# Attention, gated MLP and convolved MLP on one core: two V chunks normalised later, and the attention pairs' factors moved behind two more evictions

## The chip, the core and the metric

The kernel runs on one core of one Trainium2 chip. The metric is the device time of one execution in microseconds (us), as the median of several runs; the profile is one further execution, recorded by the hardware profiler. TensorE (PE) multiplies matrices, VectorE (DVE), ScalarE (ACT) and GpSimd (POOL) work on elements, SyncE (SP) issues most of the DMA transfers.

## What is computed

Three stages follow each other, on 4 batches of 576 positions. Attention has 8 heads of 64, a causal window of 128 positions and a linear bias. Its output, 576 x 512, goes through a gated MLP with a spatial product over the positions, and that result through a second MLP with a convolution over three positions.

```python
# attention, per batch and head
scores = where(0 <= rel < 128, q @ k.T / 8 - slope * rel, -1e9)
attn = exp(scores - max) / (sum + 1e-9)
x = attn @ v                                  # heads side by side: 576 x 512
# gated MLP
h = gelu_tanh(x @ w_in)                       # 576 x 1024
u, v = h[:, :512], h[:, 512:]
v_n = (v - mean) / sqrt(var + 1e-6) * g_ln    # over the 512 columns
v_s = w_sg @ v_n + b_sg[:, None]              # 576 x 576 product over positions
x = x + (u * v_s) @ w_out
# second MLP
h = relu(x @ w_in2)
out = (h * sigmoid(conv3(h, conv_w))) @ w_out2
```

The weights arrive as float64 and are narrowed to float32 on the chip, word by word.

## The kernel before, in words

Every float32 matrix is split into a high and a low part, and a product is made of three matmuls, high by high, high by low and low by high. A row of heads is handled two at a time, as a pair; a batch has four pairs. The attention of batch b+1 is interleaved with the gated MLP of batch b, so that PE always has something to multiply. The second MLP follows at the end and is not touched here.

The order of the work is written out by hand in `_steps()` (lines 45 to 135) as a string of short steps. A letter names the step, the numbers behind it the batch and the pair or chunk:

- `L`, `M` load q, k and V of a pair. `C` makes its scores on PE (tile `sc`) and adds the bias and takes the maximum on DVE; this is called masking here (`masked`, line 451, nine instructions to a pair, each followed by a short read of the accumulator). `E` takes the exponentials on ACT (tile `t`, nine to a pair, through `act`, line 186). `N` (`a_norm`, line 495) adds 1e-9 to the sums, takes the reciprocal on DVE (tile `r`, lines 498 and 499) and multiplies the nine blocks by it, on DVE or POOL (`scaled`, line 242). These multiplications are called the factors. `T` transposes the weights on PE (tile `pT`, 13 matmuls, line 515) and copies them out of the accumulator memory on ACT or DVE (tile `ph`). `A` multiplies them by V (tile `o`, 52 matmuls). `X` splits the result into `xg`.
- `V` (`m_v`, line 753 on) makes one of five chunks of the normalised v: matmuls (`psv`), the gelu on ACT, mean and variance on DVE (`bs`, `ba`), the reciprocal root on POOL (`rs`, lines 784 and 785), then on DVE `v` minus the mean times the root (line 786), and the split into high (ACT) and low part (DVE), tile `vn`. Chunk 4 has the last 64 positions.
- `U` makes the gate's other factor u (`psu`, then a gelu on ACT). `G` makes the product over positions (`pss`, 14 matmuls to one of four column blocks of a half), which DVE moves out with the gain and the bias (line 843, called the eviction here). POOL multiplies by u and the result is split into `gh` and `gl`. `W` multiplies by `w_out` (`pso`, 12 matmuls), and DVE adds the residual.
- `g`, `o`, `a` narrow pieces of weights: five DVE instructions (lines 324 to 331) on a tile `wa` that has two buffers, then a high part on ACT and a low part on POOL (tile `wo`) or both on POOL (`wh`, `wa`).

In the stretch that counts here the accumulator memory has two banks for `psv`, `psu`, `pss` and `pso` together and six for the attention, so the third product of a run waits until the first has been moved out. Each engine takes its instructions in the order that the scheduler leaves; `add_manual_dep` with `follow` sets an order within one engine without a wait. ACT's activations that need a table are chained in program order in this way.

The pairs of the next batch are called pair 1 to pair 4 below, the four products of the first half (256 columns) G0.0 to G0.3, and those of the second half (320 columns) G1.0 to G1.3; W0.0 to W0.3 are the output products of the first half.

Of the kernel before, what the change touches and what calls it, by code (L numbers as in the profile page):

```python
# [15 lines left out]
P = 128  # L16
# [37 lines left out]
def _steps():  # L54
# [5 lines left out]
    def scores(p):  # L60
        return [f"C{of(p)}"]
# [10 lines left out]
    def loads(p):  # L72
        return [f"L{of(p)}", f"M{of(p)}"]
# [12 lines left out]
    for b in range(B - 1):  # L86
# [5 lines left out]
        if b == 0:  # L92
            uv = ["g0", "g1", V[2], "g2", "o0.0", U[0][3], "g3", "o0.1", V[4]] + loads(p) + ["g4", "o1.0"] + scores(p) + ["o1.1", V[3], "o2.0", "o2.1"]
            uv += loads(p + 1) + U[1][:2] + ["o3.0"] + scores(p + 1) + ["o3.1"] + loads(p + 2) + U[1][2:] + scores(p + 2)
        else:
            uv = V[:2] + loads(p) + scores(p) + V[2:] + loads(p + 1) + scores(p + 1) + U[0] + loads(p + 2) + U[1][:1] + scores(p + 2) + U[1][1:]
        T, A = ([f"{x}{of(p + i)}" for i in range(4)] for x in "TA")
        gw = weigh(p) + G[0] + weigh(p + 1) + G[1][:1] + loads(p + 3) + T[:1] + G[1][1:2] + W[0][:1] + A[:1] + halves(p)
        gw += weigh(p + 2) + W[0][1:2] + T[1:2] + W[0][2:] + A[1:2] + scores(p + 3) + halves(p + 1) + weigh(p + 3) + T[2:3] + G[1][2:3]
# [35 lines left out]
def attention_gmlp_glu_kernel(  # L135
# [359 lines left out]
    def a_norm(b, m):  # L495
        s = st8[b, m]
        r = apool.tile([P, 9], F32, tag="r", name="r", bufs=2)
        nc.vector.tensor_scalar_add(r, s["sm"], 1e-9)
        nc.vector.reciprocal(r, r)
        book("dve", 170)  # L500
        for j, i in ORDER:
            e, c, _ = weights(s["t"], m, j, i)
            scaled(e, e, r[:, c : c + 1], ON["norm"])
# [39 lines left out]

    copies, masks, last_sg = [], [], []

# [203 lines left out]
    def m_v(b, j):  # L749
# [22 lines left out]
        v = mpool.tile([P, HF], F32, tag="v", name="v", bufs=NV)
        if j < 4:
            act(v, ps, AF.Gelu_apprx_tanh)
        else:
            copy(v[:r], ps[r:], True, "act")
            tt(v[:r], ps[:r], v[:r], ALU.add, "dve")
            act(v[:r], v[:r], AF.Gelu_apprx_tanh)
        bs, ba, rs = small(6, "bs"), small(2, "ba"), small(1, "rs")
        book("dve", 1200)  # L780
        nc.vector.bn_stats(bs[:r], v[:r])
        nc.vector.bn_aggr(ba[:r], bs[:r])
        book("pool", 800)
        nc.gpsimd.tensor_scalar(rs[:r], ba[:r, 1:2], 1.0, 1e-6, op0=ALU.mult, op1=ALU.add)
        nc.gpsimd.tensor_tensor(rs[:r], rs[:r], mhalf[:r], op=ALU.pow)
        nc.vector.tensor_scalar(v[:r], v[:r], ba[:r, 0:1], rs[:r], op0=ALU.subtract, op1=ALU.mult)
        split(hi[:r], lo if j < 4 else hi[64:], v[:r], "vn first")
# [39 lines left out]
    def m_sg(b, half, d):  # L827
# [44 lines left out]
    def constants(i):  # L872
# [12 lines left out]
        k=constants, l=z_load, v=z_vload, c=z_scores, e=z_exp, n=z_norm, t=z_transpose, z=z_av, j=w_in_load, L=a_load, M=a_vload, C=a_scores, E=a_exp, N=a_norm, T=a_transpose, A=a_av,  # L885
        X=a_xsplit, V=m_v, U=m_u, G=m_sg, W=m_wo, i=w_in_piece, g=w_sg_piece, o=w_out_piece, a=w2_piece,
    )
# [231 lines left out]
```

## Time and profile before

| what | value |
|---|---|
| median of 3 runs | 542.7 us |
| lowest and highest of them | 542.19 and 546.43 us |
| the profiled execution's own time | 543.29 us |
| its span, first to last instruction | 541.1 us |
| time outside the span | 2.2 us |
| mean granted TensorE clock | 0.997 of full |

PE is busy in nearly all of the span, so the time is read from the places where it isn't. The timeline merges neighbouring instructions of one kind into one row: start, length, engine, line, operation, tiles, shape and count, and in brackets how long the engine stood idle before the row and what ended that. The windows view gives, for each stretch, the busy time and count of each engine and the granted clock.

### The profile page before, as it was taken

The page shows a single profiled execution, that of the slowest core. Times are in us where ns is not written, and L with a number is a line of the kernel's source. Part 1 is how long each engine was busy: PE and PEld are TensorE (multiplying, and loading weights), DVE is VectorE, ACT ScalarE, POOL GpSimd, SP SyncE. Part 2 cuts the span into 40 slices and gives each one's busy share as a digit, 9 for nine tenths or more (in the row PEclk, how much of TensorE's full clock was granted, in tenths as well). Part 3 has the DMA queues.
Part 4 walks back from the last instruction along what each step waited for, and adds up shares of the span by engine and source line. Part 5 has one row for each costly group of instructions (what it writes and reads, how often), then busy time and mean ns, then how long its engine had stood idle before and what let it go on. Part 6 is the DMA issues. An engine that isn't in the chain of part 4 may idle for free.

```text
span 541.1 us, 11980 instructions
## 1 busy us (share of the span) xinstructions
PE 520.7 (96%) x4548; PEld 474.7 (88%) x4548; DVE 367.7 (68%) x959; ACT 258.7 (48%) x673; POOL 243.2 (45%) x383
## 2 busy tenths in 40 slices
PE   8997989999998999999999999999999999999997
PEld 6776879898898988989988999998998999999887
DVE  4999798754878875879767688687567354654300
ACT  6694578342458451376534434452554333444310
POOL 2444238542146363246453344245586545465500
PEclk9999989999999999999999999999999999999999
DMA  8974541433261765243643433902202100100011
GB/s 290 394 241 175 150 121 52 148 113 98 89 201 37 218 187 190 82 124 92 173 144 115 155 101 131 337 13 52 75 21 81 66 22 19 42 21 27 33 39 59
DMA packets 33209, 63.93 MB, mean 118 GB/s; under 512 B 3968, under 2 KB 13952, under 8 KB 33152
## 3 DMA queue, kind: packets, MB, share of 16 engines
q1 hardware_dynamic: 33008, 63.04, 35.8%
q8 instruction: 36, 0.59, 0.5%
q14 instruction: 21, 0.17, 0.1%
q10 hardware_dynamic: 144, 0.13, 0.1%
HBM read 48.47 MB, written 14.68 MB: 117 GB/s over the span
## 4 chain that ended last, share of the span: by engine, by line
PE 62%; DVE 14%; ACT 9%; POOL 7%; DMA 5%; issue 3%; SPq 0%; ACTq 0%; DVEq 0%; POOLq 0%
PE psg L213 31%; PE psv L213 7%; PE pso L213 6%; PE psu L213 5%; PE o L213 4%; ACT t L186 3%; PE pss L213 3%; PE sc L213 3%; POOL t L242 3%; PE pT L515 2%; DMA w<-in_w_in_dram 2%; DVE t L451 1%; DVE wa L330 1%; DMA kq<-in_qk_dram 1%; DVE wa L328 1%
## 5 line engine op out<-in xcount | busy, mean ns | idle before, releaser
L213 PEld LDWEIGHTS psg<-x2g,w 128*128 128x128 f32 x768 | 103.1, 188 | 2.4 <-ACT hb L973 0.7
L213 PE MATMUL psg<-x2g,w 128*128 128x256 f32 (+1 forms) x768 | 104.6, 294 | 0.6 <-ACT hb L973 0.5
L213 PE MATMUL psg<-wout,gh 128*128 128x512 f32 (+1 forms) x272 | 80.1, 378 | 0.0
L186 ACT ACTIVATE t<-t,st 128x192 f32<-128x192 f32 (+1 forms) x144 | 61.9, 431 | 15.0 <-DVE st L451 15.0
L213 PE MATMUL pss<-wsg,vn 128*128 128x256 f32 (+1 forms) x448 | 63.6, 298 | 3.6 <-DVE t L843 3.0
L213 PEld LDWEIGHTS pss<-wsg,vn 128*128 128x128 f32 x448 | 60.5, 190 | 4.7 <-DVE t L843 4.0
L977 DVE SCALAR_TENSOR_TENSOR cc<-hb,cw,cc 128x576 f32<-128x576 f32 x32 | 26.6, 832 | 46.9 <-POOL cc L242 46.9
L213 PEld LDWEIGHTS psg<-wout,gh 128*128 128x128 f32 x272 | 49.8, 188 | 8.7
L213 PE MATMUL psu<-xg,win 128*128 128x320 f32 (+1 forms) x384 | 54.2, 298 | 2.6 <-ACT win L222 1.7
L213 PEld LDWEIGHTS psu<-xg,win 128*128 128x128 f32 x384 | 51.7, 188 | 3.7 <-ACT win L222 1.8
L213 PE MATMUL pso<-gh,wo 128*128 128x256 f32 (+1 forms) x256 | 51.8, 300 | 0.5 <-DVE t L843 0.5
L213 PE MATMUL psg<-wout,gl 128*128 128x512 f32 (+1 forms) x136 | 50.9, 378 | 0.0
L213 PE MATMUL psv<-win,xg 128*128 128x512 f32 x192 | 47.6, 398 | 0.9 <-DVE wa L328 0.9
L242 POOL TENSOR_SCALAR cc<-hb,cw 128x576 f32<-128x576 f32 x32 | 28.3, 885 | 42.7 <-ACT hb L973 42.7
L451 DVE CUSTOM_DVE_ANT_0 t<-sc,tab 128x192 f32<-128x192 f32 (+1 forms) x144 | 40.4, 335 | 5.4 <-PE sc L213 5.0
L973 ACT ACTIVATE hb<-psg 128x576 f32<-128x576 f32 x32 | 20.7, 651 | 47.5 <-PE psg L213 45.0
L213 PEld LDWEIGHTS psv<-win,xg 128*128 128x128 f32 x192 | 35.5, 188 | 8.7 <-ACT win L222 1.0
L231 DVE TENSOR_TENSOR gg<-cc,hb 128x576 f32<-128x576 f32 x32 | 30.1, 943 | 17.2 <-ACT cc L186 17.0
L213 PEld LDWEIGHTS pso<-gh,wo 128*128 128x128 f32 x256 | 40.3, 188 | 1.7 <-DVE t L843 1.2
L213 PE MATMUL pso<-gl,wo 128*128 128x256 f32 (+1 forms) x128 | 36.9, 301 | 1.3 <-POOL gl L231 0.6
L231 POOL TENSOR_TENSOR t<-t,u 128x256 f32<-128x256 f32 (+1 forms) x32 | 27.2, 854 | 18.6 <-DVE t L843 18.4
L231 POOL TENSOR_TENSOR gl<-gg,gh 128x512 fp32r<-128x512 f32 x24 | 33.7, 1404 | 0.6
(101 smaller groups left out, 960.4 us busy)
## 6 DMA issues: line engine op xcount, KB each, us to landing
V<-in_v_dram SPq DMA_DIRECT2D x12, 704.0 KB, 4.7
x2s<-x2d SPq DMA_DIRECT2D x16, 288.0 KB, 2.9
w<-in_w_in_dram SPq DMA_DIRECT2D x8, 512.0 KB, 7.5
w<-in_w_out_dram SPq DMA_DIRECT2D x16, 256.0 KB, 3.2
w<-in_w_in_dram SPq DMA_DIRECT2D x16, 256.0 KB, 2.8
wout<-w2d SPq DMA_DIRECT2D x8, 512.0 KB, 6.0
q<-in_q_dram SPq DMA_DIRECT2D x12, 320.0 KB, 4.0
out_dram<-ot SPq DMA_DIRECT2D x15, 256.0 KB, 2.0
```

The lines of the kernel that those rows point to most:

```text
L186: ins = nc.scalar.activation(*args, **kw)
L213: return nc.tensor.matmul(out, lhsT, rhs, start=start, stop=stop, **kw)
L231: return (nc.vector if eng == "dve" else nc.gpsimd).tensor_tensor(dst, a, b, op=op)
L242: e.tensor_scalar(dst, src, col, 1.0, op0=ALU.mult, op1=ALU.mult)
L328: tc.keep_in_program_order(clamp.tensor_scalar(f(a), f(a), W_LOW, W_HIGH, op0=ALU.max, op1=ALU.min))
L330: nc.vector.scalar_tensor_tensor(a, high, 0xC0000000, a, op0=ALU.bitwise_and, op1=ALU.bitwise_or)
L451: nc.vector.tensor_tensor_reduce(e, bank, table, scale=-SCALE, scalar=3e38, op0=ALU.add, op1=ALU.min, accum_out=mx)
L515: ins = nc.tensor.transpose(ps[:, i * P : (i + 1) * P], src, ident)
L973: nc.scalar.activation(h[:, 1 : S + 1], ps[:, 256 : 256 + S], AF.Relu)
L977: nc.vector.scalar_tensor_tensor(cc, h[:, 0:S], cw[:, 0, c : c + 1], cc, op0=ALU.mult, op1=ALU.add)
```

## The change

Three things are done. In batch 0 the normalisation of V chunks 4 and 3 is cut out of `m_v` into a step of its own (`s`, `m_vnorm`), and both stand behind pair 2's scores; a dependency puts their first DVE instruction behind pair 2's last mask. In batches 1 and 2 the sums and reciprocals of pair 1 and pair 2 are put behind the eviction that was last in program order, that is of G0.3 and of G1.0. In the order of the steps of batches 0 to 2, `N` of pair 1 moves behind G0.3, `N` of pair 2 behind G1.0, and `T` of pair 1 behind G1.1. Lines behind the edits stand one to sixteen lower in the new file.

```diff
-            uv += loads(p + 1) + U[1][:2] + ["o3.0"] + scores(p + 1) + ["o3.1"] + loads(p + 2) + U[1][2:] + scores(p + 2)
+            uv += loads(p + 1) + U[1][:2] + ["o3.0"] + scores(p + 1) + ["s0.4", "s0.3", "o3.1"] + loads(p + 2) + U[1][2:] + scores(p + 2)
...
+        (E1, N1), (E2, N2) = (([x] for x in weigh(q)) for q in (p, p + 1))
...
-        gw = weigh(p) + G[0] + weigh(p + 1) + G[1][:1] + loads(p + 3) + T[:1] + G[1][1:2] + W[0][:1] + A[:1] + halves(p)
+        gw = E1 + G[0] + N1 + E2 + G[1][:1] + N2 + loads(p + 3) + G[1][1:2] + T[:1] + W[0][:1] + A[:1] + halves(p)
...
-        nc.vector.tensor_scalar_add(r, s["sm"], 1e-9)
+        ins = nc.vector.tensor_scalar_add(r, s["sm"], 1e-9)
+        if m < 2 and b > 0:
+            tc.add_manual_dep(ins.ins, last_gate[0].ins.name, follow, reason="behind pss")
...
+        vs[b, j] = (v, ba)
+        if b or j < 3:
+            m_vnorm(b, j)
+
+    vs = {}
+
+    def m_vnorm(b, j):
+
+        v, ba = vs.pop((b, j))
+        r = P if j < 4 else 64
...
-        nc.vector.tensor_scalar(v[:r], v[:r], ba[:r, 0:1], rs[:r], op0=ALU.subtract, op1=ALU.mult)
+        ins = nc.vector.tensor_scalar(v[:r], v[:r], ba[:r, 0:1], rs[:r], op0=ALU.subtract, op1=ALU.mult)
+        if b == 0 and j > 2:
+            tc.add_manual_dep(ins.ins, masks[0].ins.name, follow, reason="masks first")
...
-        nc.vector.scalar_tensor_tensor(t1, o, gln[:, d : d + 1], bsg[:, sl], op0=ALU.mult, op1=ALU.add)
+        last_gate[:] = [nc.vector.scalar_tensor_tensor(t1, o, gln[:, d : d + 1], bsg[:, sl], op0=ALU.mult, op1=ALU.add)]
```

The scheduler makes more of this than the text shows, so the order on the engines is given at three places. First DVE in batch 0, from the two chunks' subtraction on. `t_87` are pair 2's masks, `t_85` pair 3's, `wa` are steps of weight pieces. Before:

```order
L786 TENSOR_SCALAR v<-v,ba,rs 64x512
L330 SCALAR_TENSOR_TENSOR wa<-wst,wa 128x256
L786 TENSOR_SCALAR v<-v,ba,rs 128x512
L451 ISA t_87,st_89<-sc,tab 128x128
L451 ISA st_89 128x1
L451 ISA t_87,st_89<-sc,tab 128x192
L451 ISA st_89 128x1
L331 SCALAR_TENSOR_TENSOR wa<-wst,wa 128x256
L451 ISA t_87,st_89<-sc,tab 128x128
L451 ISA st_89 128x1
L451 ISA t_87,st_89<-sc,tab 128x192
L451 ISA st_89 128x1
```

And now, from pair 2's last mask on:

```order
L452 ISA t_87,st_89<-sc,tab 128x192
L452 ISA st_89 128x1
L800 TENSOR_SCALAR v<-v,ba,rs 64x512
L800 TENSOR_SCALAR v<-v,ba,rs 128x512
L331 SCALAR_TENSOR_TENSOR wa<-wst,wa 128x256
L330 TENSOR_SCALAR wa<-wa 128x256
L232 TENSOR_TENSOR vn<-v,vn 64x512
L332 SCALAR_TENSOR_TENSOR wa<-wst,wa 128x256
L331 SCALAR_TENSOR_TENSOR wa<-wst,wa 128x256
L232 TENSOR_TENSOR vn<-v,vn 128x512
L332 SCALAR_TENSOR_TENSOR wa<-wst,wa 128x256
L452 ISA t_85,st_90<-sc,tab 128x128
```

Two subtractions and two low parts that stood ahead of or between pair 2's masks stand behind all of them, and ahead of pair 3's.

Second ACT at the same place. Before:

```order
L222 CAST wo<-wa 128x256
L222 CAST vn<-v 64x512
L222 CAST vn<-v 128x512
L222 CAST wo<-wa 128x256
L186 ACTIVATE u<-psu 128x320 x2
L186 ACT_TABLE_LOAD
L186 ACTIVATE t_86,st_88<-t_86,st_88 128x128
L186 ACTIVATE t_86,st_88<-t_86,st_88 128x192
L186 ACTIVATE t_86,st_88<-t_86,st_88 128x128
L186 ACTIVATE t_86,st_88<-t_86,st_88 128x192 x5
L222 CAST wo<-wa 128x256
```

And now:

```order
L223 CAST wo<-wa 128x256 x2
L187 ACTIVATE u<-psu 128x320
L223 CAST vn<-v 64x512
L223 CAST vn<-v 128x512
L187 ACTIVATE u<-psu 128x320
L187 ACT_TABLE_LOAD
L187 ACTIVATE t_86,st_88<-t_86,st_88 128x128
L187 ACTIVATE t_86,st_88<-t_86,st_88 128x192
L187 ACTIVATE t_86,st_88<-t_86,st_88 128x128
L187 ACTIVATE t_86,st_88<-t_86,st_88 128x192 x4
L223 CAST wo<-wa 128x256
```

The two high parts of `vn` now stand between the last two gelus of u, directly ahead of the table load and of pair 1's exponentials (`t_86`).

Third DVE in batch 1, from the second eviction of the spatial product on (the names with numbers are the tiles that the evictions write). Before:

```order
L843 SCALAR_TENSOR_TENSOR t_2421<-pss,gln,bsg 128x256
L231 TENSOR_TENSOR gl<-t_2399,gh 128x256
L498 TENSOR_SCALAR r<-st_88 128x9
L499 RECIPROCAL r<-r 128x9
L242 TENSOR_SCALAR t_87<-t_87,r 128x192
L242 TENSOR_SCALAR t_87<-t_87,r 128x128
L242 TENSOR_SCALAR t_87<-t_87,r 128x192 x3
L224 CAST gh<-t_2421 128x256
L843 SCALAR_TENSOR_TENSOR t_2443<-pss,gln,bsg 128x256
L231 TENSOR_TENSOR gl<-t_2421,gh 128x256
L843 SCALAR_TENSOR_TENSOR t_2465<-pss,gln,bsg 128x256
```

And now:

```order
L859 SCALAR_TENSOR_TENSOR t_2409<-pss,gln,bsg 128x256
L232 TENSOR_TENSOR gl<-t_2387,gh 128x256
L225 CAST gh<-t_2409 128x256
L859 SCALAR_TENSOR_TENSOR t_2431<-pss,gln,bsg 128x256
L232 TENSOR_TENSOR gl<-t_2409,gh 128x256
L859 SCALAR_TENSOR_TENSOR t_2453<-pss,gln,bsg 128x256
L499 TENSOR_SCALAR r<-st_88 128x9
L502 RECIPROCAL r<-r 128x9
L243 TENSOR_SCALAR t_87<-t_87,r 128x192 x5
L859 SCALAR_TENSOR_TENSOR t_2496<-pss,gln,bsg 128x320
```

Pair 1's sum, reciprocal and five factors stood between the second and the third eviction, and stand behind the fourth now. Batch 2 has the same order.

On PE the 13 transpositions of pair 1 stood between G1.0 and G1.1. They now stand behind G1.1, in batch 0 behind five matmuls of `pso` too, in batches 1 and 2 with three of them before the last three transpositions; and the first two output products W0.0 and W0.1 stand wholly or nearly ahead of pair 1's product with V.

## Rows read from the trace of the kernel before

**Rows 1.** The page, part 1: busy time, share of the span and instructions of each engine.

```profile
PE 520.7 (96%) x4548; PEld 474.7 (88%) x4548; DVE 367.7 (68%) x959; ACT 258.7 (48%) x673; POOL 243.2 (45%) x383
```

**Rows 2.** Timeline of PE in batch 0, 73 to 103 us: start, length, work, idle before.

```profile
73.40 1.28 PE L213 MATMUL sc<-k,q 64*64 64x128 f32 x22
76.77 2.49 PE L213 MATMUL sc<-k,q 64*64 64x192 f32 x24 [2.09 <-DVE st L451]
...
88.88 1.58 PE L515 MATMUL pT<-ident,t 128*128 128x128 f32 x13
...
99.32 0.39 PE L213 MATMUL pso<-gl,wo 128*128 128x256 f32 x1 [0.33 <-POOL gl L231]
...
101.01 2.05 PE L213 MATMUL o<-ph,V 128*64 128x64 f32 x52
```

**Rows 3.** Windows of 5 us: busy us (count) of PE, PEld, DVE, ACT, POOL; clock, DMA.

```profile
75.00:80.00 5.00, 3.23 (x29) 3.15 (x30) 4.95 (x22) 4.99 (x19) 0.16 (x1) 0.67 0.51 169
```

**Rows 4.** Timeline of PE in batches 1 and 2, 157 to 246 us.

```profile
157.25 6.75 PE L213 MATMUL pss<-wsg,vn 128*128 128x256 f32 x56
165.87 2.32 PE L213 MATMUL pss<-wsg,vn 128*128 128x320 f32 x14 [1.87 <-DVE t L843]
...
177.92 2.05 PE L213 MATMUL o<-ph,V 128*64 128x64 f32 x52
...
193.57 2.05 PE L213 MATMUL o<-ph,V 128*64 128x64 f32 x52 [0.65 <-issue]
...
243.99 2.32 PE L213 MATMUL pss<-wsg,vn 128*128 128x320 f32 x14 [1.12 <-DVE t L843]
```

**Rows 5.** Timeline of DVE in batch 0, 70 to 83 us.

```profile
70.43 0.54 DVE L786 TENSOR_SCALAR v<-v,ba,rs 64x512 f32<-64x512 f32 x1 [0.45 <-POOL rs L785]
...
71.76 0.96 DVE L786 TENSOR_SCALAR v<-v,ba,rs 128x512 f32<-128x512 f32 x1 [0.46 <-POOL rs L785]
...
74.26 1.80 DVE L231 TENSOR_TENSOR vn<-v,vn 64x512 fp32r<-64x512 f32 x2
...
77.09 0.29 DVE L328 TENSOR_SCALAR wa<-wa 128x256 f32<-128x256 f32 x1
77.30 0.35 DVE L451 CUSTOM_DVE_ANT_0 t<-sc,tab 128x192 f32<-128x192 f32 x1
...
79.85 0.28 DVE L451 CUSTOM_DVE_ANT_0 t<-sc,tab 128x128 f32<-128x128 f32 x1
...
82.21 0.17 DVE L498 TENSOR_SCALAR r<-st 128x9 f32<-128x9 f32 x1
...
82.55 0.42 DVE L843 SCALAR_TENSOR_TENSOR t<-pss,gln,bsg 128x256 f32<-128x256 f32 x1
```

**Rows 6.** Timeline of POOL in batch 0, 71 to 100 us.

```profile
71.69 0.75 POOL L231 TENSOR_TENSOR wo<-wa,wo 128x256 fp32r<-128x256 f32 x1
...
82.74 4.20 POOL L242 TENSOR_SCALAR t<-t,r 128x128 f32<-128x128 f32 x9 [1.42 <-DVE r L499]
...
96.73 2.54 POOL L231 TENSOR_TENSOR gl<-t,gh 128x256 fp32r<-128x256 f32 x3
```

**Rows 7.** Timeline of ACT in batch 0, 74 to 80 us.

```profile
74.66 1.28 ACT L186 ACT_TABLE_LOAD   x1
75.96 0.40 ACT L186 ACTIVATE t<-t,st 128x128 f32<-128x128 f32 x1
...
79.37 0.39 ACT L222 CAST wo<-wa 128x256 fp32r<-128x256 f32 x1
```

**Rows 8.** The chain that ended last, in batches 1 and 2: start, length, work.

```profile
159.20 3.96 ACT t L186 x18
163.65 1.58 DVE t L242 x5
...
237.32 3.96 ACT t L186 x18
```

**Rows 9.** Timeline of ACT in batch 1, behind the last exponential of pair 3.

```profile
171.06 1.04 ACT L222 COPY ph<-pT 128x512 f32<-128x512 f32 x2
```

More of the change, by code (lines that the diff above doesn't have):

```diff
@@ L542, in a_transpose @@
         s["ph"] = (p0, p1, pc)
-    copies, masks, last_sg = [], [], []
+    copies, masks, last_sg, last_gate = [], [], [], []
     def product(x, half, work, waits=(), first=False, scale=False):
@@ L764, in m_v @@
             mm(ps[:rows], a, w, start=n == 0, stop=n == len(work) - 1, skip_group_check=j == 4)
+        v = mpool.tile([P, HF], F32, tag="v", name="v", bufs=NV)
+        if j < 4:
+            act(v, ps, AF.Gelu_apprx_tanh)
+        else:
+            copy(v[:r], ps[r:], True, "act")
+            tt(v[:r], ps[:r], v[:r], ALU.add, "dve")
+            act(v[:r], v[:r], AF.Gelu_apprx_tanh)
+        bs, ba = small(6, "bs"), small(2, "ba")
+        book("dve", 1200)
+        nc.vector.bn_stats(bs[:r], v[:r])
+        nc.vector.bn_aggr(ba[:r], bs[:r])
+        vs[b, j] = (v, ba)
[5 more added lines that the diff above has]
+        r = P if j < 4 else 64
         if j < 4:
@@ L771, in m_v @@
             hi = lo = mpool.tile([P, HF], F32R, tag="vt", name="vn", bufs=1)
[L772 to L782, printed above, removed]
+        rs = small(1, "rs")
         book("pool", 800)
@@ L885, in attention_gmlp_glu_kernel @@
         k=constants, l=z_load, v=z_vload, c=z_scores, e=z_exp, n=z_norm, t=z_transpose, z=z_av, j=w_in_load, L=a_load, M=a_vload, C=a_scores, E=a_exp, N=a_norm, T=a_transpose, A=a_av,
-        X=a_xsplit, V=m_v, U=m_u, G=m_sg, W=m_wo, i=w_in_piece, g=w_sg_piece, o=w_out_piece, a=w2_piece,
+        X=a_xsplit, V=m_v, s=m_vnorm, U=m_u, G=m_sg, W=m_wo, i=w_in_piece, g=w_sg_piece, o=w_out_piece, a=w2_piece,
     )
```

## The prediction, made before the changed kernel ran

> **What bounds the kernel now.** The page comes first: PE is busy 96% of the span [rows 1], so other engines count only where PE stands still or runs slowly. The timeline of PE shows where that is among the places which the change touches. In batch 0, PE waits 2.09 us in the middle of pair 3's scores for DVE's masks, and the windows view shows what follows: between 75 and 80 us the granted clock is 0.67 on average, that is about 3.3 us at 1.2 instead of 2.4 GHz [rows 2, 3]. A little later PE picks its way through W0.0 behind POOL's low parts, until pair 2's product with V begins at 101.01 [rows 2]. From there to batch 1's products PE has no gap. In batches 1 and 2 the first product of the second half waits 1.87 and 1.12 us for an eviction, and pair 3's product with V waits 0.65 us in batch 1, with the same wait again in batch 2 [rows 4]. That makes 4.29 us to be had in batches 1 and 2. In batch 0 the work from 73.40 to 101.01 would take about 20 us without hindrance, by estimate: six products of the positions 11.0 at the pace of batch 1 [rows 4], two transpositions of 1.4 and a product with V of 2.0 [rows 2], and some 4.5 for the scores and 24 matmuls of `pso`. So some 7 of its 27.6 us could be had there at most.
>
> **Batches 1 and 2.** The eviction for which PE waits is late because DVE first does pair 1's reciprocal and five factors, 1.58 us [rows 8]. They now stand behind the fourth eviction, so G1.0 follows G0.3 at once: 165.87 less 1.87 is 164.0, and in batch 2 it is 242.87 [rows 4]. What is late next is found by following the same work on. From the start of G1.0 to pair 2's product with V before, PE worked 12.05 us without a gap (165.87 to 177.92), on G1.0, G1.1, both transpositions, 24 matmuls of `pso` and pair 1's product [rows 4]. The new order has the same pieces, with pair 1's product (about 2.0 us) and pair 2's transpositions (1.4) last, so PE comes to pair 1's product after 8.7 us, at 172.7 in batch 1. That product needs four copies of the transposed weights, and all four stand on ACT behind the 27 exponentials now; two stood on DVE. ACT started the exponentials at 159.20; nine take 3.96, so 27 with one cast between are done at about 171.1, which is where the copies start before [rows 8, 9]. One cast of 0.3, one short copy of 0.25 and three of 0.5 (sized from the two in 1.04) later it is 173.2. So 0.5 of the 1.87 is lost again, and batch 1 keeps 1.37. In batch 2 the exponentials start at 237.32 [rows 8], 5.55 before G1.0's new start and not 4.8 as in batch 1, so PE comes 0.75 later to the same copies: that wait is nothing there, and it keeps 1.12. DVE's part moves behind evictions that it does early enough; the cover is POOL, which has the other four factors done before PE ends G1.1.
>
> The 0.65 at pair 3's product is DVE bringing the copies out late. Ahead of them DVE now has three more weight steps net (two pieces are bunched and delayed), about 0.6 us, but pair 4's masks, which used to wait for weight steps, start about that much earlier against PE. Its bounds are 0 and 0.65 for each batch; I take 0.3, the middle. Of the transfers, V for pairs 3 and 4 stands no longer behind the writes of a weight piece on SP's queue; k and q of the next batch stand behind two pieces' writes, with some 20 us to spare. Sum of the two batches: 1.37 + 0.3 + 1.12 + 0.3 = 3.1 us.
>
> **Batch 0.** The two chunks' steps on DVE (0.54 and 0.96 with waits of 0.45 and 0.46, then 1.80) stand ahead of pair 2's last mask, which ends at about 77.6 [rows 5]. Without these 4.2 us it would end at 73.4. It doesn't, since two weight steps come up sooner among the masks, each the first of a new piece, and each needs a buffer that POOL's low part frees: the one at 71.69 lasts 0.75 [rows 6], the next follows at once, to 73.2. One weight step of 0.2, then five masks at 0.28 and two more steps of 0.2 [rows 5] end at 75.2. PE can run pair 3's scores nearly without a pause, as these need only the sixth and the eighth mask. The 2.09 goes, but its place is taken.
>
> The subtractions now end at 75.7 and 76.2 (0.5 each). ACT's casts of the high parts stand ahead of the last gelu of u: two of 0.5, the gelu with 0.4 (sized from the 0.39 of a 256-column cast), then the table load of 1.28 [rows 7]. So pair 1's exponentials start at 78.4, not at 75.96, 2.4 us later. PE meanwhile reaches the products at about 75.1, stops at the fourth chunk until the low parts come (78.6), and ends G0.0 at 79.
>
> G0.2 needs G0.0's eviction. Ahead of that DVE has pair 3's masks (2.36 from 79.85 to 82.21; now 78.9 to 81.2 [rows 5]) and one weight step which waits for POOL, which waits for a cast that stands on ACT behind seven exponentials: 78.4 + 3.0 + 0.4, POOL 0.75, the step 0.2 make 82.8, and the eviction ends at 83.2. Before, it ended at 82.97 [rows 5]. The first 10 us thus gain nothing. After it G0.2 to G1.1 run without a wait: two products at 1.69 (56 matmuls took 6.75), two at 2.1 [rows 4], to 91.0.
>
> Pair 1's transpositions need nine factors on POOL. POOL has a low part ahead of them whose high part ACT makes behind 21 exponentials and two casts, at about 88.3; 0.75 for the low part and 4.20 for the nine [rows 6] make 93.2. PE waits about 1.7 us for that. Then 1.4 of transpositions, the copies on ACT up to 96.0, pair 1's product to 98.0, pair 2's transpositions to 99.3 and the eight matmuls of `pso` that are left: pair 2's product starts at about 100.5. POOL's last low part, 99.3 before [rows 6], is done at 99. Gain: 101.0 less 100.5, 0.5 us. Every us by which ACT starts its exponentials sooner or later moves this by as much, so I keep as bounds a gain of 3 and a loss of 1.5.
>
> The subtraction of 0.96 beside POOL's low part, against 0.54 when POOL was at a single column [rows 5, 6], shows that the two get in each other's way. The Trainium skill (SBUF — State Buffer, section "SBUF: two separate sides") says that VectorE and GpSimd share a pair of ports which one instruction holds to its end while the other stands still; this pair of rows agrees. By that rule POOL's nine factors, beside DVE's factors now, could take longer than before, where DVE had weight steps beside them; the 4.20 of the row has such company in it already, and the sum goes by the row.
>
> **Sum.** 0.5 + 3.1 = 3.6 us. The profiled execution took 543.29 in all (541.1 span and 2.2 around it), so it would take 539.7; it lies 0.6 above the median of the runs, 542.7, so against that 539.1. Behind batch 2 the chain starts from PE, and nothing there is changed, so what is gained before arrives at the end.
>
> **The rivals.**
> *Faster.* Batch 0 gives more: if POOL's low parts do not hold DVE's weight steps, pair 2's masks end at 73.4, the exponentials start at 76.6, and the whole chain behind ACT moves 1.8 us forward; batches 1 and 2 lose nothing at the copies and all of the 0.65 goes. Gain 2.3 + 4.29 = 6.6, time 536.1. For it: most of batch 0's loss is a chain of small waits, and shortening one link can draw in several. Against it: the row of POOL's low part at 71.69.
> *No change.* The waits only move: PE stops at pair 1's product in batches 1 and 2 for as long as it no longer stops at G1.0, since the copies hang on ACT, which is busy without a gap up to 171.06 [rows 8, 9], and the 0.65 stays. Batch 0 gains the 0.5. Time 542.2. For it: ACT's end is only 0.5 us from deciding it by my own count.
> *Slower.* The clock in batch 0: G0.0 stops twice (at the fourth chunk's high and low part), G0.2 stops for its bank, and if the clock stays at 1.2 GHz as it did after 2.09 us of waiting [rows 2, 3], G0.1, G0.2 and G0.3 take 3.4 instead of 1.7 each. G0.3 then ends at 90.0 rather than 86.7, POOL's factors start at 91.0 rather than 89.1, and batch 0 loses 1.5 instead of gaining 0.5. That is slower as a whole only with the waits of the rival before in batches 1 and 2: 544.2. It decides from the point at which batches 1 and 2 together give less than the 1.5 that batch 0 loses. The Trainium skill (TensorE: Matmul & The Clock Gate, section "A second HAM failure mode: psum-queue depth-cycling") tells of a kernel in which short stops between groups of matmuls pull the clock down again and again, which would be this case; the trace shows the clock falling once, behind the longest of the stops here, and no repetition.
>
> **How the numbers follow.** The forecast gets 0.45, faster 0.24, no change 0.21, slower 0.10. The range runs from 535.4 (all of the 4.29 and the 3 us of batch 0's upper bound) to 544.2 (the slower rival, batch 0 at its lower bound). One per cent is 5.4 us, about what a measurement of this kernel can tell from no change. A gain of over 5.4 needs the faster rival or the forecast's upper edge: 0.28. Slower by that much needs the slower rival and more, which I have not found: 0.06. Within it 0.66.
>
> **What would show it.** In the changed kernel's trace: no wait at G1.0 in batches 1 and 2, and one of up to 0.6 us at pair 1's product, ended by ACT's copies; no 2.09 in pair 3's scores of batch 0, but a stop of over 1 us inside G0.0; the exponentials of pair 1 at about 78.4; and pair 2's product with V in batch 0 within 1 us of 100.5. If the exponentials start before 77 or pair 2's product stands at 99 or earlier, batch 0 is wrong; if PE still waits over 1 us between G1.0 and pair 1's product, batches 1 and 2 are.

## The result, and the profile after

The change makes the kernel slower: 551.06 us against 543.78 (medians of 6 runs each), a ratio of 1.013, interval 1.010 to 1.016. The forecast was 539.1, with a range up to 544.2. The profiled execution took 551.25 us, with a span of 549.1 against 541.1. PE's busy time rose by 1.1 us only [rows 1]; the rest is waits. The page, part 1, of the kernel after:

```profile
PE 521.8 (95%) x4548; PEld 475.8 (87%) x4548; DVE 366.3 (67%) x957; ACT 258.9 (47%) x676; POOL 242.9 (44%) x382
```

Where the 8.0 us of the span come from is read from the start of each stretch, that is PE's first V chunk (`psv`) or first G product (`pss`) of a batch:

| PE's first | before | after | later by | added here |
|---|---|---|---|---|
| V of batch 1 (end of batch 0) | 126.02 | 131.41 | 5.39 | 5.39 |
| G of batch 1 | 157.25 | 162.64 | 5.39 | 0 |
| V of batch 2 | 204.15 | 209.81 | 5.66 | 0.27 |
| G of batch 2 | 236.01 | 242.56 | 6.55 | 0.89 |
| V of batch 3 | 282.25 | 289.91 | 7.66 | 1.11 |
| end of span | 541.1 | 549.1 | 8.0 | 0.34 |

**Batch 0.** PE's timeline, answering to [rows 2]:

```profile
73.74 2.39 PE L214 MATMUL sc<-k,q 64*64 64x128 f32 x46
75.83 1.36 PE L214 MATMUL pss<-wsg,vn 128*128 128x256 f32 x9
77.49 0.50 PE L214 MATMUL pss<-wsg,vn 128*128 128x256 f32 x2 [0.30 <-ACT vn L223]
79.42 3.52 PE L214 MATMUL pss<-wsg,vn 128*128 128x256 f32 x17 [1.43 <-DVE vn L232]
84.03 1.91 PE L214 MATMUL pss<-wsg,vn 128*128 128x256 f32 x14 [1.09 <-DVE t L859]
86.31 1.92 PE L214 MATMUL pss<-wsg,vn 128*128 128x256 f32 x14 [0.37 <-DVE t L859]
88.87 4.38 PE L214 MATMUL pss<-wsg,vn 128*128 128x320 f32 x28 [0.64 <-DVE t L859]
...
96.20 2.21 PE L518 MATMUL pT<-ident,t 128*128 128x128 f32 x13 [2.36 <-POOL t L243]
...
100.84 2.04 PE L214 MATMUL o<-ph,V 128*64 128x64 f32 x52
...
106.40 1.82 PE L214 MATMUL o<-ph,V 128*64 128x64 f32 x46 [1.03 <-DVE ph L225]
```

The 2.09 us in pair 3's scores are gone. In their place come two stops in G0.0, one at each bank that G0.2, G0.3 and G1.0 need, and 2.36 us at pair 1's transpositions. DVE and POOL show what those waited for, answering to [rows 5] and [rows 6]; first the timeline of DVE:

```profile
83.28 0.29 DVE L325 TENSOR_SCALAR wa<-wst 128x256 uint32<-128x256 uint32 x1 [1.22 <-POOL wo L232]
83.49 0.48 DVE L859 SCALAR_TENSOR_TENSOR t<-pss,gln,bsg 128x256 f32<-128x256 f32 x1
...
84.21 0.78 DVE L330 TENSOR_SCALAR wa<-wa 128x256 uint32<-128x256 uint32 x1
85.02 0.84 DVE L331 SCALAR_TENSOR_TENSOR wa<-wst,wa 128x256 uint32<-128x256 uint32 x1
...
89.95 0.47 DVE L859 SCALAR_TENSOR_TENSOR t<-pss,gln,bsg 128x256 f32<-128x256 f32 x1
90.35 0.15 DVE L499 TENSOR_SCALAR r<-st 128x9 f32<-128x9 f32 x1
```

and that of POOL:

```profile
84.09 0.74 POOL L232 TENSOR_TENSOR wo<-wa,wo 128x256 fp32r<-128x256 f32 x1 [0.84 <-ACT wo L223]
84.78 0.79 POOL L232 TENSOR_TENSOR t<-t,u 128x256 f32<-128x256 f32 x1
...
90.50 0.74 POOL L232 TENSOR_TENSOR t<-t,u 128x256 f32<-128x256 f32 x1 [0.76 <-DVE r L499]
91.20 0.74 POOL L232 TENSOR_TENSOR wo<-wa,wo 128x256 fp32r<-128x256 f32 x1
91.93 4.22 POOL L243 TENSOR_SCALAR t<-t,r 128x128 f32<-128x128 f32 x9
```

The eviction of G0.3 is over at 90.4, and pair 1's sum `r` may come only behind it. ("The change" names batches 1 and 2 for this rule. But `b > 0` in the code counts the batch of the attention, which runs one ahead, so the rule acts in the G and W stretch of batch 0 too.) On POOL the multiplication by u that follows that eviction and one low part of a weight piece come first, and the nine factors start at 91.93 instead of 82.74 [rows 6]. The clock falls twice, where [rows 3] had one fall; the windows view, 2 us each, with the clock in the third column from the right:

```profile
80.00:82.00 2.00, 2.00 (x12) 2.00 (x11) 2.00 (x16) 2.00 (x11) 0.00 (x0) 0.51 0.93 313
82.00:84.00 2.00, 0.94 (x5) 0.64 (x4) 0.79 (x5) 2.00 (x11) 0.73 (x1) 0.64 0.18 69
...
98.00:100.00 2.00, 2.00 (x9) 1.71 (x9) 1.34 (x4) 1.11 (x3) 2.00 (x6) 0.50 0.00 0
```

**Batches 1 and 2.** The waits of 1.87 and 1.12 us at G1.0 [rows 4] are gone, and six products run as one row. But others have come. PE's timeline in batch 1 and at the first G product of batch 2, and under it DVE's in both batches:

```profile
196.79 0.56 PE L214 MATMUL pso<-gh,wo 128*128 128x320 f32 x2 [1.36 <-DVE t L859]
...
198.63 2.05 PE L214 MATMUL o<-ph,V 128*64 128x64 f32 x52 [0.40 <-issue]
...
204.21 2.04 PE L214 MATMUL o<-ph,V 128*64 128x64 f32 x52 [0.77 <-ACT ph L223]
...
242.56 10.97 PE L214 MATMUL pss<-wsg,vn 128*128 128x256 f32 x84 [1.35 <-DVE st L452]
```

```profile
194.46 0.29 DVE L325 TENSOR_SCALAR wa<-w 128x256 uint32<-128x256 uint32 x1 [2.64 <-DMA w2d<-wa]
...
274.57 0.30 DVE L325 TENSOR_SCALAR wa<-w 128x256 uint32<-128x256 uint32 x1 [2.90 <-DMA w2d<-wa]
```

Between pair 4's masks and the eviction of G1.3, DVE starts a weight piece. Its tile `wa` was the source of a DMA (`w2d`) which two bunched pieces had sent out just before, so the step waits 2.64 us. Pair 4's `r`, the eviction of G1.3 and the copies of the transposed weights are queued behind it. The 0.89 us at G of batch 2 are a longer wait for pair 3's masks, 1.35 instead of 0.48 us; ahead of these masks too stands a weight step that waits 1.02 us for `w2d`, but one did before (0.89), and what makes them late isn't shown.

The mean granted clock differs between executions of one and the same kernel and the span with it (in the 29 runs of the kernel before beside e13 to e15, 540.2 to 541.7 us at a clock of 0.996 or above and 545.2 to 546.1 at 0.987 or below), so times are compared by medians and intervals, and a profile, which is one execution, by its rows of waits.

### The profile page after: what moved, and what is told of

The parts are those of the page before. It is cut to its first block, busy times and chain, and to the rows that moved or that the text cites. A ratio compares the mean times of both kernels' runs of the same rounds, so it can differ in the third digit from the quotient of the medians.

```text
span 549.1 us, 11984 instructions
## 1 busy us (share of the span) xinstructions
PE 521.8 (95%) x4548; PEld 475.8 (87%) x4548; DVE 366.3 (67%) x957; ACT 258.9 (47%) x676; POOL 242.9 (44%) x382
## 4 chain that ended last, share of the span: by engine, by line
PE 51%; DVE 18%; ACT 10%; POOL 8%; issue 7%; DMA 6%; SPq 0%; POOLq 0%; ACTq 0%; DVEq 0%
PE psg L214 30%; PE pso L214 5%; ACT t L187 5%; PE psv L214 5%; PE pss L214 3%; POOL t L243 3%; PE psu L214 3%; PE o L214 2%; DMA w2d<-wa 2%; DVE t L452 2%; PE sc L214 2%; PE pT L518 1%; DVE wa L331 1%; DVE wa L330 1%; DMA w<-in_w_in_dram 1%
## 5 line engine op out<-in xcount | busy, mean ns | idle before, releaser
L214 PE MATMUL pso<-gh,wo 128*128 128x256 f32 (+1 forms) x256 | 53.2, 305 | 3.8 <-DVE t L859 3.8
```

Source lines behind the costliest of these rows:

```text
L214: return nc.tensor.matmul(out, lhsT, rhs, start=start, stop=stop, **kw)
```

## The experiments

Seventeen kernels ran, each beside the kernel before. The ratio is worked out from all runs and is not the quotient of the two medians.

| run | what it is | median | before | ratio (95%) |
|---|---|---|---|---|
| e1 | V part alone | 546.47 | 543.00 | 1.0051 (1.0015 to 1.0086) |
| e2 | new order in batch 0 alone | 547.22 | 543.00 | 1.0072 (1.0049 to 1.0094) |
| e3 | new order in batches 1, 2 alone | 547.82 | 543.00 | 1.0085 (1.0055 to 1.0116) |
| e4 | change without V part | 548.97 | 543.00 | 1.0104 (1.0071 to 1.0137) |
| e5 | change, piece buffer free earlier | 553.04 | 543.38 | 1.0170 (1.0111 to 1.0229) |
| e6 | before, piece buffer free earlier | 544.99 | 543.38 | 1.0009 (0.9973 to 1.0046) |
| e7 | change, no rule on `r` in batch 0 | 546.41 | 543.38 | 1.0043 (1.0011 to 1.0075) |
| e8 | e4 with e5 and e7 | 545.12 | 543.38 | 1.0021 (0.9989 to 1.0054) |
| e9 | change, three pieces moved back | 550.51 | 544.32 | 1.0129 (1.0093 to 1.0165) |
| e10 | e4 with e7 | 546.07 | 544.32 | 1.0039 (1.0013 to 1.0064) |
| e11 | e10 with e9 | 545.52 | 544.32 | 1.0024 (0.9998 to 1.0050) |
| e12 | e10, two pieces among V and U | 559.46 | 544.32 | 1.0299 (1.0265 to 1.0333) |
| e13 | e11, fifth piece at the end | 547.55 | 544.82 | 1.0046 (1.0020 to 1.0071) |
| e14 | e13, first two pieces spaced | 547.52 | 544.82 | 1.0058 (1.0031 to 1.0085) |
| e15 | e14 with the V part | 548.17 | 544.82 | 1.0058 (1.0035 to 1.0081) |
| e16 | e13 with e5 | 545.49 | 543.33 | 1.0033 (1.0008 to 1.0058) |
| e17 | e14 with e5 | 546.62 | 543.33 | 1.0044 (1.0017 to 1.0070) |

**e1 to e4: the parts alone.** e3 keeps the new order in batches 1 and 2 only, and undoes the V part:

```diff
+        if b == 0:
+            gw = weigh(p) + G[0] + weigh(p + 1) + G[1][:1] + loads(p + 3) + T[:1] + G[1][1:2] + W[0][:1] + A[:1] + halves(p)
...
-        if m < 2 and b > 0:
+        if m < 2 and b > 1:
...
-        if b or j < 3:
-            m_vnorm(b, j)
+        m_vnorm(b, j)
...
-        if b == 0 and j > 2:
-            tc.add_manual_dep(ins.ins, masks[0].ins.name, follow, reason="masks first")
```

With it go the two steps `s0.4` and `s0.3`. e2 has the opposite conditions (`if b:` and `b == 1`), e1 the old order everywhere with the V part kept, e4 the V part undone and nothing else.

> Only the V part (the last two V chunks of batch 0 scaled behind the second pair's masks); the order of pairs, G, T and factors is that of before in all batches. Theory 1 (in batch 0 the V part makes pair 1's exponentials about 3 us late, and only the new place of r behind the eviction of G0.3 turns that into a loss): nine factors of pair 1 on POOL near 86 instead of 82.74, pair 1's transpositions wait 0 to 1.5 us, no change in batches 1 and 2, time 542.5 to 545.0 beside a before of about 543.5. Theory 2 (the stops of G0.0 and the clock at 1.2 GHz behind them cost on their own): G0.0 to G1.0 run at a mean clock under 0.7 and the time is 546 to 549.

> Only batch 0 has the new order of pairs, G, T and factors; its V chunks and batches 1 and 2 are as before. Theory 1 (late exponentials and late r are needed together): exponentials on time at 75.96, r of pair 1 near 88, its nine factors near 88 to 92, pair 1's transpositions wait under 1 us: 542.5 to 545.0. Theory 2 (the order alone puts the nine factors behind the transpositions' slot): 547 to 549, with a wait of over 2 us at pair 1's transpositions.

> Only batches 1 and 2 have the new order; batch 0 is as before. Theory 1 (the order wins about 1.5 us in each of the two batches up to pair 4's scores and gives it back to the weight piece's step that waits for the DMA out of its buffer): 543.5 to 546.0, with a wait of 2 us or more on the DMA w2d of a wa buffer on DVE in batch 1. Rival, the forecast on record: no such wait, 540.4, that is 3.1 under before.

> The change without its V part: new order in batches 0, 1 and 2, V chunks as before. Theory 1: batch 0 costs 0 to 1.5, batches 1 and 2 cost 1 to 2.5 together: 544.5 to 547.5. Theory 2 (the order alone loses the 5 us of batch 0): 549 to 551.

My theory 1, that batch 0's loss needs both parts, fell: e1 and e2 lie in the ranges of theory 2, e4 at its edge. In the profiles, batch 0 ends 2.3 us later than before in e1, 3.35 in e2 and 1.8 in e4. The V part alone gives the stops in G0.0 and the fall of the clock; PE's timeline of e1, and a window behind it:

```profile
79.38 3.18 PE L214 MATMUL pss<-wsg,vn 128*128 128x256 f32 x17 [1.43 <-DVE vn L232]
84.22 6.96 PE L214 MATMUL pss<-wsg,vn 128*128 128x256 f32 x42 [1.65 <-DVE t L859]
91.01 1.58 PE L518 MATMUL pT<-ident,t 128*128 128x128 f32 x13
```

```profile
84.00:86.00 2.00, 1.78 (x8) 1.78 (x9) 1.93 (x6) 2.00 (x10) 2.00 (x5) 0.50 0.00 0
```

The transpositions wait for nothing there. The order alone (e2) does the other half, as does e4. PE's timeline of e2, and of e4 with a window behind it:

```profile
94.74 3.02 PE L520 MATMUL pT<-ident,t 128*128 128x128 f32 x13 [2.44 <-POOL t L245]
```

```profile
94.39 1.64 PE L518 MATMUL pT<-ident,t 128*128 128x128 f32 x13 [2.40 <-POOL t L243]
...
97.22 2.04 PE L214 MATMUL o<-ph,V 128*64 128x64 f32 x52
```

```profile
96.00:98.00 2.00, 2.00 (x30) 1.84 (x30) 1.31 (x4) 1.17 (x4) 2.00 (x6) 1.00 0.00 0
```

This pair gives the price of a fall of the clock. In e4's profiled execution (545.90 us; its median is 548.97) the clock stayed at 1.00 behind the wait, and from the transpositions to pair 1's product took 2.83 us. In the changed kernel, with the same order from there on and the clock down to 0.50, it took 4.64.

e3 has the wait on `w2d` in both batches (2.26 and 2.46), so it isn't a consequence of batch 0, and its G1.0 waits for nothing. Its median is above the range of theory 1, and its profile doesn't hold all of that: batch 0, whose steps are ordered as in the kernel before, ended 1.5 later, with the clock at 0.50 from 100 to 102. The parts don't add up either: by the medians 3.5, 4.2 and 4.8 us make 12.5, and the whole costs 7.3. In the profiles, counting for each part only the batches that it changes up to V of batch 3, 2.3, 3.35 and 0.95 make 6.6 of the change's 7.66.

**e7: the rule on `r` in batch 0.**

```diff
-        if m < 2 and b > 0:
+        if m < 2 and b > 1:
```

> The changed kernel without the rule that holds r of pairs 1 and 2 behind the eviction of G0.3 and G1.0, in batch 0 only. Theory 1 (the rule puts pair 1's nine factors 9 us later on POOL, and its transpositions wait): nine factors near 86 instead of 91.93, the wait of 2.36 at pair 1's transpositions and the 1.03 at pair 2's product go, the second stretch at 1.2 GHz (96 to 102) goes too: 545.5 to 548.0. Theory 2 (the later exponentials of the V part and the weight steps slowed beside POOL set the time of the transpositions): they still wait, 549 to 552.

Theory 1 holds. POOL starts on the factors at 83.39, the transpositions wait for nothing, and the clock falls once. The wait at pair 2's product is halved (0.53) rather than gone, and pair 1's product now waits 0.84. V of batch 1 begins at 126.4 instead of 131.41, and the ratio goes from 1.0130 to 1.0043. PE's timeline of e7, and POOL's:

```profile
91.92 1.58 PE L518 MATMUL pT<-ident,t 128*128 128x128 f32 x13
```

```profile
83.39 1.75 POOL L243 TENSOR_SCALAR t<-t,r 128x128 f32<-128x128 f32 x4 [0.71 <-DVE r L502]
```

**e5, e6, e8: the buffer.** Both parts of a piece stay in its staging tile, of which there are three, and the buffer is free when POOL is done:

```diff
-            hi, lo = pool.tile([P, 256], F32R, tag="wh", name="wh", bufs=2), a.bitcast(F32R)
+            hi, lo = (kept["st"][:, 256 * h : 256 * h + 256].bitcast(F32R) for h in range(2))
...
-        a = narrowed(src, 256, pool, "wa", 2, pool, "w64", 2, bool(p2pool))
+        a = narrowed(src, 256, pool, "wa", 2, pool, "w64", 2 if p2pool else 3, bool(p2pool))
```

> The changed kernel, with the two parts of a w2 weight piece left in the piece's staging tile (three of these instead of two, the wh tiles gone), so that the piece's buffer wa is free as soon as POOL has its low part, and not only when the DMA out of it is done. Same room. Theory 1 (DVE's step that waits for the DMA holds r of pair 4 and the eviction of G1.3): the waits of 2.64 and 2.90 us on DMA w2d go, W1.1's wait (1.36 and 1.57), pair 3's product (0.40) and pair 4's product (0.77) go or halve, 545.5 to 548.0. Rival (the wait only names what came last; the staging load or POOL comes as late): the waits move, 549.5 to 552.

> The kernel before with the same edit of the piece's tiles and nothing else. Theory 1: before has such a wait only behind the V chunks (1.26 and 0.89 us) where TensorE waits for nothing: no change, 542.0 to 544.5. Rival (the edit brings something of its own): 1 us or more below before.

> The order of batches 1 and 2 of the change, without the V part, without the rule on r in batch 0, with the piece's tiles of e5. Theory 1: batch 0 costs 0 to 1, batches 1 and 2 gain the 1.4 each that the change's profile shows up to pair 4's scores and keep it: 540 to 543. Rival (something else in the second half of batches 1 and 2 takes the gain): 544 to 548.

e5 lies 1 us above the range of its rival (553.04, from four runs). Its profile is of little help for the time, as it is 3.8 us late in G0.0 of batch 0 already (81.25 for 77.49). In it the wait on `w2d` is gone from that place, but pair 3's product waits 1.45 and 0.70 us instead of 0.40, and in batch 2 a piece waits 1.15 for its load. e8 lies in its rival's range (545.12). In batch 1 of its profile the piece waits longest for its load; in batch 2 that wait doesn't come. DVE's timeline of e8, and what PE then waits for:

```profile
193.03 1.67 DVE L326 TENSOR_SCALAR wa<-w 128x256 uint32<-128x256 uint32 x1 [3.36 <-DMA w<-in_w_out_dram]
```

```profile
196.25 3.04 PE L214 MATMUL o<-ph,V 128*64 128x64 f32 x44 [4.89 <-issue]
```

The row says "issue", but the product starts as DVE's copies `ph` end (196.15), and these stood behind the weight step. So I no longer asked which DMA is late, but where the piece stands in DVE's queue; e9 tests that. e6, the control, shows no change in its time (the interval holds 1). But in its profile the V and U stretch of batch 2 takes 33.78 us (before: 31.86), with DVE waiting 5.20 us for POOL's root where it waited 2.70 before. So the tiles can bring a cost of their own (the stretch takes 33.86 in e5 and 32.34 in e8), and these runs don't show what an earlier free buffer alone is worth.

**e9 to e12: the pieces' places.** The same six pieces, three of them further back; e12 leaves four there (behind `A[0]`, `G[1][3]`, `A[3]` and `W[1][2]`) and gives two to the V and U stretch:

```diff
-            s += ["B1"] + weave(uv, now[:4]) + ["B0"] + weave(gw, now[4:])
+            s += ["B1"] + weave(uv, now[:4])
+            for x, y in zip(now[4:], (G[1][0], A[0], G[1][3], A[3], W[1][1], W[1][3])):
+                gw.insert(gw.index(y) + 1, x)
+            s += ["B0"] + gw
```

> The changed kernel with three of the six w2 pieces of the G and W stretch of batches 1 and 2 moved back: the third and fourth, which stand on DVE between pair 4's masks and the copies behind G1.3's eviction, go behind G1.3 and behind pair 4's product, the fifth behind W1.1. Nothing else. Theory 1, now put as: whatever DMA it waits for (out of its buffer in the change, into its staging tile in e5), a weight step ahead of r and of G1.3's eviction on DVE's queue is what gives batches 1 and 2 their loss: W1.1 (1.36, 1.57), pair 3's product (0.40) and pair 4's product (0.77) wait for nothing or under 0.3, each of the two batches is 2 to 2.7 us shorter, 545.5 to 548.5. Rival (these places wait for POOL's eight factors and the exponentials in any case): W1.1 or the two products wait as long as before, 549.5 to 552.

> The change without the V part and without the rule on r in batch 0; batches 1 and 2 as in the change. Theory 1: batch 0 within 0.7 of before at pair 2's product, batches 1 and 2 cost 0 to 1.5 together: 543 to 546. Rival (batch 0 loses by the moved transpositions alone): 546 to 549.

> e10 with the pieces of e9. Theory 1: 2 to 2.7 per batch under e10 in its profile, 539 to 542. Rival: no more than 1 under e10, 543 to 546.

> e10 with four pieces in the G and W stretch instead of six (behind pair 1's product, G1.3, pair 4's product and W1.2) and six instead of four in the V and U stretch. Theory 1: as e11 in the G and W stretch, and the two pieces cost nothing in the V and U stretch because TensorE does not wait for DVE there: 538.5 to 542. Rival (six pieces wait for their DMA among the V chunks and make vn or the scores late): 543 to 547, with waits on DVE v or st of over 1 us.

The waits at W1.1 and at the products of pairs 3 and 4 are gone in e9 and e11, in both batches; in e9 DVE comes to the eviction of G1.3 at 193.95, for 196.19 in the changed kernel. That is theory 1's mechanism, but the times are those of the rivals, since the next piece in the row took over. In e11 the fifth piece's step waits for its buffer ahead of the last `pso` evictions, and the next V chunks wait for those. DVE's timeline, and PE's:

```profile
201.84 0.29 DVE L328 TENSOR_SCALAR wa<-w 128x256 uint32<-128x256 uint32 x1 [1.58 <-DMA w2d<-wa]
```

```profile
204.44 5.76 PE L217 MATMUL psv<-win,xg 128*128 128x512 f32 x17 [2.43 <-DVE x L235]
```

e10, the base without batch 0's part, is still 2.1 us behind by its ratio (546.07, the edge between its two ranges). In its profile batch 0 ends at 125.1, 0.9 ahead of before, so the rival, that the moved transpositions cost batch 0 something, falls. Batch 2 loses it, with a wait of 1.66 for pair 3's masks (`st`) at its first G and the waits on `w2d`; 0.9 more is lost behind V of batch 3.

e12 is the same fault, larger, in a third place, and its time lies above both of its ranges. Two bunched pieces at the end of the V and U stretch put a waiting step ahead of G0.0's eviction, and the kernel loses 15 us. DVE's row, and PE's:

```profile
166.39 0.29 DVE L328 TENSOR_SCALAR wa<-w 128x256 uint32<-128x256 uint32 x1 [5.29 <-DMA w2d<-wa]
```

```profile
167.14 9.56 PE L217 MATMUL pss<-wsg,vn 128*128 128x256 f32 x56 [6.93 <-DVE t L859]
```

**e13 to e17: does the order pay once they are out of the way?** e13 changes `W[1][1]` in the edit above to `W[1][3]`; e14 also begins with `A[0], W[0][3]`; e15 is e14 with the V part; e16 and e17 have e5's tiles.

> e11 with its fifth piece moved on from W1.1 to behind W1.3, beside the sixth, so that no weight step stands ahead of the last two pso evictions of a batch. Theory 1 (in e11 the fifth piece's step waited 1.58 us for the DMA out of its buffer, and the next batch's first V chunk 2.43 and 1.74 for the evictions behind it): these two waits go, batches 1 and 2 are 2 to 3 shorter in the profile than in e10, no wait of TensorE of over 0.6 between the V chunks and the next ones, 539.5 to 542.5. Rival (the next V chunks' vn and masks become late in place of it): 543.5 to 547, with waits on DVE v or vn of over 1 us in the V and U stretch.

> e13 with its first two pieces, which in the change come together behind pair 2's product, spaced out: behind pair 1's product and behind W0.3. Theory 1: as e13 or up to 1 below it, 539 to 542.5. Rival (the first piece's steps now stand ahead of W0.1's and pair 2's copies and make these late): 543 to 546.

> e14 with the V part of the change put back. Theory 1 (the V part costs what it did in e7 against e10, 0.3 to 1.3 us): 540 to 543.5. Rival (with the rule gone the V part brings its half microsecond of the forecast): 538.5 to 541.5, under e14.

> e13 with the piece's tiles of e5 (both parts left in one of three staging tiles, the buffer free without the DMA). Theory 1 (the G and W stretch of batch 1 is 2.8 shorter in e13 and the V and U stretch 4.2 longer, behind a weight step's wait of 4.12 for the DMA out of its buffer): that wait falls under 2, the waits of 2.03 and 1.85 of TensorE behind it under 0.6, 540.5 to 544.5. Rival (the pieces go through load, steps and DMA no faster, and the step waits for its staging load instead, as in e5): 545.5 to 551, with a wait of 2 us or more on the load of a w2 piece in a G and W or V and U stretch.

> e14 with the same tiles. Theory 1: 540.5 to 544.5, and no wait on a staging load over 1 us. Rival, as in e16: 545.5 to 551.

In the G and W stretches the order pays: 44.2 us each in e13 (159.6 to 203.8 and 239.8 to 284.0) against 46.90 and 46.24 before. But the V and U stretch between takes 36.0 instead of 31.86. In e13 DVE waits there for a piece's buffer, and PE behind it, here and once more (1.85) at the first G of batch 2:

```profile
210.40 0.29 DVE L328 TENSOR_SCALAR wa<-w 128x256 uint32<-128x256 uint32 x1 [4.12 <-DMA w2d<-wa]
```

```profile
225.99 4.76 PE L217 MATMUL psu<-xg,win 128*128 128x256 f32 x36 [2.03 <-DVE v L235]
```

In e16, with the tiles, the buffer is free, and POOL is late instead: it waits ahead of its copies for V chunk 4, then has two pieces' parts, and only then the root that the first V chunk needs. POOL's timeline, and DVE's:

```profile
208.91 0.73 POOL L229 TENSOR_SCALAR xt<-xg 128x128 fp32r<-128x128 f32 x2 [7.22 <-DMA x2d<-x]
```

```profile
212.97 0.55 DVE L803 TENSOR_SCALAR v<-v,ba,rs 128x512 f32<-128x512 f32 x1 [6.41 <-POOL rs L802]
```

PE's wait for `v` there is 1.95, much as in e13, so the rival of e16 was right in its time (to 0.01) and wrong in its place. e17 lies in that range too (546.62).

The rest of the loss stands in a fourth place, batch 3. At V of batch 3, e16's profile is at 281.48 and e17's at 281.12, 0.8 and 1.1 us ahead of before (282.25). From there to the end of the span before takes 258.9 us, and e13 to e17 take 262.7 to 264.3. In batch 3 the eviction of G0.0 stands on DVE behind eight weight steps, before and in e16. The first of them waits for ACT, in e16 until 309.93 for 306.36 before; so the eviction comes 3.6 us later, and with it the low parts `gl` of W0.0, for which PE waits up to 2.01 us. DVE's timeline before and in e16, and PE's in e16:

```profile
306.36 0.29 DVE L328 TENSOR_SCALAR wa<-wa 128x256 f32<-128x256 f32 x1 [1.86 <-ACT wa L322]
...
309.77 0.47 DVE L843 SCALAR_TENSOR_TENSOR t<-pss,gln,bsg 128x256 f32<-128x256 f32 x1
```

```profile
309.93 0.29 DVE L333 TENSOR_SCALAR wa<-wa 128x256 f32<-128x256 f32 x1 [2.40 <-ACT wa L327]
...
313.39 0.48 DVE L860 SCALAR_TENSOR_TENSOR t<-pss,gln,bsg 128x256 f32<-128x256 f32 x1
```

```profile
320.68 0.58 PE L217 MATMUL pso<-gl,wo 128*128 128x256 f32 x1 [2.01 <-DVE gl L235]
```

No run tests a kernel without this. e13 and e14 lie half a us and 1.5 us above their rivals' ranges; e14's mechanism is that of e13 (a wait of 4.19 on the buffer), not late copies in W0. e15's ranges both rested on a base that didn't come, and beside e14 the V part makes no difference that these intervals show. No version beats the kernel before; the nearest, e8 and e11, can't be told from it.

What stays open: whether a placing of all ten pieces of a batch, and of those that batch 3 works on, exists in which the 2 to 2.7 us per batch are kept. A third `wa` buffer beside the two staging tiles was not tried.

## Why the prediction was wrong

- **Pair 3's scores, G0.0, the exponentials: right.** No wait in the scores, a stop of over 1 us inside G0.0 (1.43), exponentials at 79.08 for 78.4 (0.33 of the difference is there at 51 us already, ahead of the first place that the change touches). G0.0's eviction ends at 84.0 for 83.2.
- **"After it G0.2 to G1.1 run without a wait ... to 91.0": the step that failed in batch 0.** G0.2, G0.3 and G1.0 waited 1.09, 0.37 and 0.64 for evictions. I had counted no weight step between these evictions and sized one elsewhere at 0.2; there are nine, and five of them took 0.72 to 0.84 us, each beside an operation of POOL on two tensors. I had hung POOL's factors on a low part whose cast came nearly when I said (89.0 for 88.3). What held them was the eviction of G0.3 with `r` behind it, and the multiplication by u ahead of them on POOL. They start at 91.93, not 89.1, and the transpositions at 96.20, not 93.2. e7 takes the rule away, and 5.0 us of batch 0 with it in its profile.
- **From the transpositions to pair 2's product: a second step that failed in batch 0.** The sum had 7.3 us for it (93.2 to 100.5), with no wait and the full clock; it took 10.20. The clock made 1.8 of the difference (4.64 against e4's 2.83), and pair 2's product waited 1.03 for DVE's copies, a term that I had put at nothing. Together with the 3.0 us by which the transpositions came late, that makes the difference between a gain of 0.5 and a loss of 5.39.
- **The clock: wrongly left out of the sum.** I gave it to the slower rival at 0.10. It fell in 80 to 84 and again behind the 2.36, in 96 to 102, which is the repetition that I had said the trace didn't show. That agrees with what I cited from the Trainium skill (TensorE: Matmul & The Clock Gate, section "A second HAM failure mode: psum-queue depth-cycling") in so far as the falls come behind stops between groups of matmuls; but not every such stop brings one, as e4's 2.40 shows. The slower rival priced the wrong fall: G0.3 ended at 88.2, not at its 90.0, and the 1.8 us were lost behind the transpositions, by the second fall. And a fall costs only where PE has nothing else to wait for. The one that I started from [rows 3] cost the kernel before nothing: e3 has the same wait of 2.09 us in pair 3's scores with the clock at 1.00 behind it, then waits 1.55 us for G0.0's eviction instead, and comes to pair 1's transpositions at 88.81, for 88.88 before. So the clock was no part of the 7 us that I thought batch 0 could give. e3's rows:

```profile
76.00:80.00 4.00, 3.31 (x42) 3.27 (x43) 3.97 (x22) 4.00 (x19) 0.23 (x1) 1.00 0.38 143
```

```profile
82.95 6.01 PE L216 MATMUL pss<-wsg,vn 128*128 128x256 f32 x42 [1.55 <-DVE t L858]
```

- **The wait at G1.0 in batches 1 and 2: right.** It is gone in both, and pair 4's scores start 1.48 sooner against G in batch 1 (I had 1.37) and 0.88 in batch 2 (I had 1.12). The wait "of up to 0.6 us at pair 1's product" came as 0.47 at W0.1 instead (176.44 in batch 1), for the eviction of G1.1. So the sign that I had named for batches 1 and 2 (no wait of over 1 us between G1.0 and pair 1's product) was met, and they lost all the same, further on.
- **"The 0.65 at pair 3's product ... I take 0.3": the step that failed in batches 1 and 2.** I had seen the two bunched pieces and counted them as DVE time (0.6 us). What costs is that the next piece's first step waits for the DMA that empties its buffer, 2.64 and 2.90 us, with the eviction of G1.3 behind it on the queue. W1.1, pair 3's and pair 4's products then wait 1.36 + 0.40 + 0.77 = 2.5 in batch 1, where pair 3's and pair 4's had waited 0.65 + 0.19 before. e9 shows it: with these steps moved, these waits go. I had followed the transfers on SP's queue, but not what a transfer still holds.
- **The stretch between batches 1 and 2: put at nothing, and 0.89.** The longer wait for pair 3's masks at G of batch 2 is in no term of the sum.
- **"Nothing there is changed": nearly right.** Behind batch 2 the profile adds 0.34.

## What to carry to other kernels

An instruction that may wait for a DMA must not stand in an in-order queue ahead of one that TensorE waits for; when work is moved, ask for each filler that shares the queue which transfer still reads the buffer it will write. Making that buffer free earlier or moving the filler only helps if the filler's whole way, its load, its steps and its write, fits where it is put; else the wait appears at the next place, as it did here in e8, e11, e12 and e13, and in batch 3 of e16 and e17. And a rule that holds one step behind another sets a time that moves with everything ahead of it: with it the new order gained 1.5 us at first in batch 1, and it cost 5 us in batch 0, where the evictions were late.

## What was not expected of the hardware

- The same wait at the same place may or may not be followed by a fall of the clock. Behind the 2.09 us in pair 3's scores it was 0.67 on average from 75 to 80 in the kernel before [rows 3], and 1.00 from 76 to 80 in e3. Behind the 2.4 at pair 1's transpositions it fell in e2 (0.55 from 94 to 96) and stayed at 1.00 in e4. The 1.87 at G1.0 of batch 1 left it at 1.00 in the kernel before; in e1 a wait of 1.86 there was followed by 0.50. The windows view of e2 and of e1 (e3's and e4's stand above):

```profile
94.00:96.00 2.00, 1.26 (x6) 1.26 (x7) 1.93 (x5) 0.52 (x2) 2.00 (x4) 0.55 0.00 0
```

```profile
170.00:172.00 2.00, 2.00 (x10) 1.96 (x10) 1.97 (x8) 2.00 (x11) 1.57 (x4) 0.50 0.00 0
```

- DVE's steps on 128 x 256 words take 0.28 to 0.42 us alone and 0.72 to 0.84 when they start while POOL works on two tensors: in the rows of the kernel after, the steps at 84.21 and 85.02 end 0.16 and 0.29 us behind POOL's operations from 84.09 and 84.78. That agrees with the shared ports of the Trainium skill (SBUF — State Buffer, section "SBUF: two separate sides"); I had weighed that rule for POOL's factors and not for DVE's own steps.
